# Releasing loads at two points of a step, one-hot rows queued by step, and narrower weight subtractions, in a fused attention and expert kernel

## The chip, the cores and the metric

The kernel runs on one core of a Trainium2 chip. The core has five engines with a queue each: PE (matrix multiplies and transposes, results in eight PSUM banks ps0 to ps7), DVE (vector work), ACT (activations and copies), POOL (the general engine, which also issues indirect DMAs) and SP (which here only issues DMAs). Every queue runs in its own order; an instruction that has to wait holds up all that stand behind it on the same engine. The metric is the device time of one execution in microseconds (us); lower is better.

## The reference

Eight batches, eight heads, 512 local and 32 global tokens, head size 64. Local tokens attend to a window of 32 to each side and to the global ones; global tokens attend to all. The result, 4352 tokens of width 512, goes into a mixture of eight experts with a "sticky" choice: a token takes its own best expert when its local gate is under 0.5, otherwise that of the token before.

```python
    s_g = scale * np.matmul(q_g, k_all.transpose(0, 1, 3, 2))
    out_g = np.matmul(sm(s_g), v_all)
    s_ll = scale * np.matmul(q_l, k_l.transpose(0, 1, 3, 2))
...
    mask = np.abs(pos[:, None] - pos[None, :]) <= window
    s_ll = np.where(mask, s_ll, -1000000000.0)
...
    s_l = np.concatenate([s_lg, s_ll], axis=-1)
    a_l = sm(s_l)
    out_l = np.matmul(a_l, np.concatenate([v_g, v_l], axis=2))
...
            fresh_e = int(np.argmax(logits[b, s]))
            if s == 0 or local_gate[b, s] < 0.5:
                e = fresh_e
            else:
                e = prev_e if prev_e >= 0 else fresh_e
...
            h = np.maximum(x[b, s] @ w1[e], 0.0)
            out[b, s] = p[e] * (h @ w2[e])
```

## The kernel before

**Attention.** `Attn.run` walks 48 units in 48 steps s = 0 to 47. A batch is six units: l0, l1, g0, l2, g1, l3, where an l unit is a pair of heads for the local tokens and a g unit is the global tokens of two pairs. A step starts unit s (scores, maximum, subtraction, exponential) and finishes unit s - 2 (transposes of the exponentials, product with v, division). In the order in which a step is written: the loads, `prep`, the transposes of unit s - 2 (`l_t` or `g_t`, L264 and L332), some pieces of the gate computation of earlier batches, the scores of unit s (`l_s`, L247, in two halves; or `g_s`, L300) with the maxima, and the product with v (`l_av`, `g_av`, L280 and L343). The order of the text is the order on each engine.

**Loads.** At the top of an l step, `load` (L178) fetches q and k of the pair two ahead into the ring `raw` of four buffers, and `loadv` (L188) fetches v of the next pair into the ring `v` of four. SP issues them in order; each waits only until its buffer is free, so SP can run ahead of the steps. `prep` makes the tiles `qbd` and `kx` of the next pair from `raw` with six instructions on POOL (L191). These tiles have two buffers, so `prep` of a pair waits for the scores of the pair two before it.

**Routing.** Small instructions of the routing come from generators that `drip` advances between the instructions of a step. `stage_a` handles the first five batches (CA = 21 columns of 128 tokens) while attention still runs: it ranks the tokens by expert, and builds in `low` one one-hot row block of 128x128 for each column in the tile `o1` (printed as o). POOL makes all 21 (L916), in the order in which `drip` comes to them. `pick` then multiplies the 21 blocks with a second one-hot table on PE (L1013), which gives the list idx of rows that the first expert blocks gather.

**Experts.** A weight is used as a sum of two parts: `split` makes the upper one by a cast on ACT (L1164, `hi`), `flush` the lower one by a subtraction (L1174, `lo`), 1024 columns wide. The first two weights of the first block are subtracted on POOL, in `pre` during the last steps of attention; all others on DVE. `mm1` multiplies hi with the upper part of x, lo with it, and hi with the lower part of x, 12 matmuls of 128x256 into one PSUM bank from the ring `ph`; `early` runs the first NX = 3 blocks, in the first of which the leftovers of attention (the generator `tail`: transposes L332, products L343, L280) are interleaved. The ring `ph` starts with ps2; ps0 to ps2 are also the banks of the attention scores, ps3 is the bank of the gate pieces. `ps_63` to `ps_70` in the listings below are ps0 to ps7. Behind that come eleven and more expert blocks of the same kind.

## Time and profile before

| | |
|---|---|
| median of 3 runs | 690.34 us (688.4 to 693.82) |
| the profiled execution | 690.5 us |
| its span, first to last instruction | 688.8 us |
| PE busy, share of the span | 659.1 us, 96% |
| DVE, ACT, POOL busy | 425.9, 343.0, 212.0 us |
| mean granted PE clock | 0.984 |
| attention ends, expert blocks begin | about 224 us |

The profile names engines, lines of the source and tiles. Columns of a timeline are start and length in us, engine, line, operation, out<-in, shapes and count; in brackets stands how long the engine was idle before and what ended that. Rows of time windows give busy us of PE, weight loads (PEld), DVE, ACT and POOL, then the granted PE clock, the busy share of the DMA engines and GB/s. A row of waits gives total us, times, and the longest.

### The profile page before, as it was taken

How to read it: one execution, taken by the hardware profiler on the slowest of the kernel's cores; microseconds unless marked ns; L12 is line 12 of the kernel's file. 1: busy time of each engine (PE TensorE's matmuls, PEld its weight loads, DVE VectorE, ACT ScalarE, POOL GpSimd, SP SyncE). 2: the span in 40 equal slices, each digit the busy share in tenths (PEclk: the TensorE clock that was granted, in tenths of full speed). 3: DMA queues.
4: the chain of work that ended last, by engine and by line, in shares of the span. 5: the costliest groups of instructions: out<-in, count | busy, mean ns of one | idle time of the engine just before them, and what ended most of it. 6: DMA issues, size and time to landing. Idle time of an engine off the chain costs nothing.

```text
span 688.8 us, 18451 instructions
## 1 busy us (share of the span) xinstructions
PE 659.1 (96%) x7253; PEld 566.6 (82%) x7253; DVE 425.9 (62%) x1050; ACT 343.0 (50%) x614; POOL 212.0 (31%) x342
## 2 busy tenths in 40 slices
PE   8999999999979799998998999999999999999995
PEld 7788788877767788887887988889898889888994
DVE  7878787777877777994517636325354516255573
ACT  4565565664646474653326635344444325255563
POOL 7734434343674211132022403040403020133023
PEclk9999999999999899999998999999999999999998
DMA  8957977979576486878319547347466417265673
GB/s 334 362 210 258 335 257 276 346 279 332 177 285 227 158 309 234 264 247 277 125 60 320 196 161 244 101 130 230 149 213 194 146 57 230 68 227 177 226 272 103
DMA packets 43012, 151.45 MB, mean 220 GB/s; under 512 B 7965, under 2 KB 9245, under 8 KB 38688
## 3 DMA queue, kind: packets, MB, share of 16 engines
q1 hardware_dynamic: 30928, 118.25, 49.4%
q0 software_dynamic: 6960, 21.90, 9.6%
q10 hardware_dynamic: 4896, 8.80, 3.5%
q8 instruction: 78, 1.28, 0.8%
q14 instruction: 150, 1.23, 0.6%
HBM read 130.55 MB, written 19.69 MB: 218 GB/s over the span
## 4 chain that ended last, share of the span: by engine, by line
PE 80%; DVE 10%; POOL 4%; issue 4%; ACT 1%; POOLq 0%; ACTq 0%; DVEq 0%
PE ps L1276 27%; PE ps L1265 25%; PE ps L247 7%; PE ps L264 4%; PE ps L280 3%; PE ps L1219 3%; PE ps L300 2%; POOL o L916 2%; PE ps L356 2%; PE ps L343 2%; DVE wp L1174 2%; PE ps L332 1%; DVE wq L1174 1%; PE ps L371 1%; PE ps L236 1%
## 5 line engine op out<-in xcount | busy, mean ns | idle before, releaser
L1282 POOL DMA_INDIRECT out_dram<-y,tk x39 | 42.9, 1100 | 315.1 <-ACT y L1281 232.7
L1276 PE MATMUL ps<-wp,wq 128*128 128x512 f32 x504 | 129.5, 404 | 1.0 <-ACT wq L1379 1.0
L1276 PEld LDWEIGHTS ps<-wp,wq 128*128 128x128 f32 x504 | 94.1, 192 | 21.3 <-ACT wq L1379 1.3
L1265 PE MATMUL ps<-wp,wp 128*128 128x256 f32 (+5 forms) x672 | 109.3, 322 | 0.3 <-issue 0.3
L1265 PEld LDWEIGHTS ps<-wp,wp 128*128 128x128 f32 x672 | 103.6, 188 | 5.3 <-issue 0.4
L1268 DVE SCALAR_TENSOR_TENSOR wq<-ps,wq 128x256 fp32r<-128x256 f32 (+5 forms) x80 | 41.7, 525 | 73.8 <-ACT wq L1267 66.4
L1267 ACT ACTIVATE wq<-ps 128x256 fp32r<-128x256 f32 (+5 forms) x80 | 37.3, 469 | 79.1 <-PE ps L1265 69.4
L1222 DVE TENSOR_TENSOR wp<-ps,wp 128x512 fp32r<-128x512 f32 x40 | 27.6, 691 | 78.3 <-ACT wp L1221 78.2
L191 POOL TENSOR_SCALAR_AFFINE_SELECT qbd<-raw 64x512 f32<-64x512 f32 x62 | 44.4, 715 | 89.1 <-PE ps L247 69.7
L247 PE MATMUL ps<-kx,qbd 128*64 128x128 f32 x1024 | 65.9, 280 | 3.9 <-POOL kx L191 3.5
L247 PEld LDWEIGHTS ps<-kx,qbd 128*64 128x64 f32 x1024 | 56.6, 139 | 11.8 <-POOL kx L191 6.7
L1281 ACT ACTIVATE y<-ps,pp 128x512 f32<-128x512 f32 x39 | 26.9, 689 | 77.7 <-PE ps L1276 70.7
L252 DVE TENSOR_REDUCE mx<-ps 128x4 f32<-128x512 f32 x64 | 43.8, 685 | 32.0 <-PE ps L247 32.0
L258 ACT ACTIVATE pe<-pe 128x512 f32<-128x512 f32 x64 | 40.8, 638 | 43.3 <-DVE pe L254 43.3
L1174 DVE TENSOR_TENSOR wp<-raw,wp 128x1024 fp32r<-128x1024 f32 x47 | 56.9, 1217 | 2.9 <-ACT wp L1164 2.8
L1205 POOL DMA_INDIRECT xa<-xs,idx x42 | 52.3, 1245 | 16.3 <-issue 10.0
L1164 ACT CAST wp<-raw 128x1024 fp32r<-128x1024 f32 x49 | 50.9, 1047 | 2.7 <-DVE f L930 1.5
L1221 ACT CAST wp<-ps 128x512 fp32r<-128x512 f32 x40 | 23.4, 588 | 53.2 <-PE ps L1219 53.2
L254 DVE TENSOR_TENSOR pe<-ps,mx 128x512 f32<-128x512 f32 x64 | 43.9, 686 | 1.0
L191 POOL TENSOR_SCALAR_AFFINE_SELECT kx<-raw 128x384 f32<-128x384 f32 (+3 forms) x127 | 43.2, 373 | 2.9 <-DMA raw<-in_qk_dram 0.8
L266 ACT COPY pt<-ps 128x512 f32<-128x512 f32 x64 | 34.7, 600 | 9.8 <-PE ps L264 9.1
L280 PEld LDWEIGHTS ps<-v,pt 128*32 128x32 f32 x2048 | 32.0, 110 | 9.2 <-issue 6.5
(280 smaller groups left out, 1182.5 us busy)
## 6 DMA issues: line engine op xcount, KB each, us to landing
raw<-in_w_dram SPq DMA_DIRECT2D x78, 512.0 KB, 4.3
v<-in_vw_dram SPq DMA_DIRECT2D x32, 1040.0 KB, 7.9
raw<-in_qk_dram SPq DMA_DIRECT2D x32, 528.0 KB, 7.5
xa<-in_w_dram SPq DMA_DIRECT2D x26, 512.0 KB, 4.7
xT<-in_w_dram SPq DMA_DIRECT2D x20, 512.0 KB, 5.3
xs<-xa ACTq DMA_DIRECT2D x8, 1056.0 KB, 8.6
qgb<-in_qg_dram SPq DMA_DIRECT2D x8, 128.0 KB, 5.0
xa<-xs,idx POOLq DMA_INDIRECT x42, 4.9
```

The lines of the kernel that those rows point to most:

```text
L191: self.nc.gpsimd.affine_select(out=out, in_=in_, pattern=pat, compare_op=ALU.is_ge, fill=0.0, base=0, channel_multiplier=0)
L247: nc.tensor.matmul(sp[64 * t2:64 * t2 + 64, t], qbd[:, w], kf[:, f:f + P], start=False, stop=True, skip_group_check=True)
L252: nc.vector.tensor_reduce(out=mx, in_=st["sps"][hb], axis=AX.X, op=ALU.max)
L254: nc.vector.tensor_tensor(out=st["pe"][:, 4 * hb:4 * hb + 4], in0=st["sps"][hb], in1=mx.broadcast_to([P, 4, P]), op=ALU.subtract)
L280: nc.tensor.matmul(o[32 * w4:32 * w4 + 32, g, h], pt[:, 2 * g + w4 // 2, w4 % 2, h, :], v[:, w, h * (D + 1):(h + 1) * (D + 1)], start=True ...
L1164: nc.scalar.copy(out=hi, in_=raw)
L1174: (nc.gpsimd if pool else nc.vector).tensor_tensor(out=lo, in0=raw, in1=hi.bitcast(F32), op=ALU.subtract)
L1205: self.nc.gpsimd.indirect_dma_start(out=self.xr[j] if k == "early" else self.xr4[:, j], out_offset=None, in_=src, in_offset=bass.IndirectO ...
L1265: nc.tensor.matmul(ph, a[:, dc, fs], b_[:, dc, n0:n1], start=(n == 0), stop=(n == 11))
L1268: nc.vector.scalar_tensor_tensor(out=hl[:, fc, n0:n1], in0=ph, scalar=0.0, in1=hh[:, fc, n0:n1].bitcast(F32), op0=ALU.max, op1=ALU.subtract)
L1276: nc.tensor.matmul(py, a[:, fc, js], b_[:, fs], start=(fc == 0 and k == 0), stop=(fc == 7 and k == 2))
L1282: sc = nc.gpsimd.indirect_dma_start(out=self.out, out_offset=bass.IndirectOffsetOnAxis(ap=self.g[1][:, j:j + 1], axis=0), in_=y, in_offset ...
```

## The change

Five edits are in it.

1. `get` issues the loads of q, k and of v and, where `gate` is set, makes them wait for one PE instruction. The load of q and k of the pair two ahead now stands behind the transposes of the step and waits for the last of them; that of v of the next pair stands behind the first half of the scores and waits for its last matmul. SP's order of instructions stays as it was; each such row has one more wait, for PE.
2. Of the 21 one-hot blocks, the first CD = 6 are made on DVE, three in one instruction; the other 15 go in five entries of three into a list `pq`. A step takes one entry from it (a g step two) and puts it on POOL behind `prep`. `pick` does not go on to its matmuls until the list is empty.
3. The two subtractions on POOL are cut into four of 256 columns each.
4. The ring `ph` starts with ps3 in place of ps2.
5. `rt.pq` and `at.pq` are the same list.

```diff
 NX = 3
+CD = 6
 LISTS = "lists"
...
         self.cur = {}
+        self.gate = self.last = None
+        self.pq = []
         self.gens = []
...
     def load(self, b, pr):
-        nc = self.nc
         if pr == 0:
             self.cur[b] = {"v": []}
         c = self.cur[b]
         t = c[("qk", pr)] = self.ld()
-        nc.sync.dma_start(t, self.qk[b, pr])
+        self.get(t, self.qk[b, pr])
 
     def load_g(self, b):
         g = self.cur[b]["qg"] = self.qgb()
         self.nc.sync.dma_start(g, self.qg[b])
 
     def loadv(self, b, pr):
-        nc = self.nc
         v = self.v()
         self.cur[b]["v"].append(v)
-        nc.sync.dma_start(v.rearrange("p w c -> p (w c)"), self.vw[b, pr])
+        self.get(v.rearrange("p w c -> p (w c)"), self.vw[b, pr])
+
+    def get(self, out, in_):
+        d = self.nc.sync.dma_start(out, in_)
+        if self.gate is not None:
+            self.tc.add_manual_dep(d.ins, self.gate.ins.name, mybir.DependencyInfo(mybir.DependencyClass.Sync, mybir.DependencyReason.DATA), reason="pace")
 
...
                 f = 32 * (3 * (w // 2) + w % 2)
-                nc.tensor.matmul(sp[64 * t2:64 * t2 + 64, t], qbd[:, w], kf[:, f:f + P], start=False, stop=True, skip_group_check=True)
+                self.last = nc.tensor.matmul(sp[64 * t2:64 * t2 + 64, t], qbd[:, w], kf[:, f:f + P], start=False, stop=True, skip_group_check=True)
 
...
         for i in range(4):
-            nc.tensor.transpose(tp[:, i], st["pe"][:, 4 * hb + i], self.cst.idf)
+            self.last = nc.tensor.transpose(tp[:, i], st["pe"][:, 4 * hb + i], self.cst.idf)
         pt = self.pt()
...
             for i in range(3):
-                nc.tensor.transpose(tp[:, i], st["pg"][:, c0 + i], self.cst.idf)
+                self.last = nc.tensor.transpose(tp[:, i], st["pg"][:, c0 + i], self.cst.idf)
             nc.scalar.copy(out=pt[:, c0:c0 + 3], in_=tp[:, 0:3])
...
             sg = st is not None and not sl
+            ahead = pairs[npr + 1:npr + 3] if nl else []
             if nl:
-                if npr + 2 < len(pairs):
-                    b, i = pairs[npr + 2]["u"]
-                    self.load(b, i)
-                    if i == 0:
-                        self.load_g(b)
-                if npr + 1 < len(pairs):
-                    self.loadv(*pairs[npr + 1]["u"])
                 npr += 1
                 if npr < len(pairs):
                     self.prep(pairs[npr])
+            for _ in range(2 - nl):
+                if self.pq:
+                    self.pq.pop(0)()
             if sl:
                 self.l_t(st, 0)
                 self.l_t(st, 1)
             if sg:
                 self.g_t(st)
+            self.gate = self.last
+            if len(ahead) > 1:
+                b, i = ahead[1]["u"]
+                self.load(b, i)
+                if i == 0:
+                    self.load_g(b)
             if nl:
...
                 self.l_s(nx, 0)
+                self.gate = self.last if s > 0 else None
+                if ahead:
+                    self.loadv(*ahead[0]["u"])
                 self.l_max(nx, 0)
...
         yield from self.rank2(0, CA)
-        for c0 in range(0, CA, 3):
-            yield from self.low(c0, min(c0 + 3, CA), True)
+        for c0 in range(0, CD, 3):
+            yield from self.low(c0, c0 + 3, False)
+        for c0 in range(CD, CA, 3):
+            self.pq.append(lambda c0=c0: all_(self.low(c0, min(c0 + 3, CA), True)))
         yield PSUM
...
         yield from lag(wait)
+        while self.pq:
+            yield
         yield PSUM
...
         self.add([buf.tile([P, 2048], F32R, name=f"wp{k}") for k in range(2)])
-        self.ph, self.py, self.xtp = Ring(ps[2:4]), Ring(ps[0:2]), Ring(ps[4:6])
+        self.ph, self.py, self.xtp = Ring([ps[3], ps[2]]), Ring(ps[0:2]), Ring(ps[4:6])
         self.xt0 = None
...
             pool, raw, hi, lo = self.pend.pop(0)
-            (nc.gpsimd if pool else nc.vector).tensor_tensor(out=lo, in0=raw, in1=hi.bitcast(F32), op=ALU.subtract)
+            m = 4 if pool else 1
+            for k in range(m):
+                f = slice(1024 // m * k, 1024 // m * (k + 1))
+                (nc.gpsimd if pool else nc.vector).tensor_tensor(out=lo[:, f], in0=raw[:, f], in1=hi[:, f].bitcast(F32), op=ALU.subtract)
             if not any(raw is x for x in self.gone):
...
     at.at1, at.at2 = s1, s2
+    rt.pq = at.pq
     at.run(rt, moe)
```

Line numbers of the changed file are 6 to 19 higher in the places below. On POOL, around the seventh batch (raw_80 holds its fourth pair, raw_77 the first of the eighth batch), the order before is:

```order
L191 AFFINE_SELECT kx_146<-raw_79 128x7x32
L916 TENSOR_SCALAR o_290<-io_261,plo 128x128 [waits DVE_49]
L916 TENSOR_SCALAR o_290<-io_261,plo 128x128 x11
L191 AFFINE_SELECT qbd_145<-raw_80 64x16x32 [waits DMAHW5_49,PE_49]
L191 AFFINE_SELECT qbd_145<-raw_80 64x16x32 [waits Pool_49]
L191 AFFINE_SELECT kx_147<-raw_80 128x128 [waits Pool_49]
L191 AFFINE_SELECT kx_147<-raw_80 128x6x64
L191 AFFINE_SELECT kx_147<-raw_80 128x32
L191 AFFINE_SELECT kx_147<-raw_80 128x7x32
L916 TENSOR_SCALAR o_290<-io_261,plo 128x128 x9
L191 AFFINE_SELECT qbd_144<-raw_77 64x16x32 [waits DMAHW7_49,PE_49]
```

And now:

```order
L197 AFFINE_SELECT kx_147<-raw_80 128x7x32
L930 TENSOR_SCALAR o_290<-io_261,plo 128x128 [waits DVE_49]
L930 TENSOR_SCALAR o_290<-io_261,plo 128x128 x5
L197 AFFINE_SELECT qbd_144<-raw_77 64x16x32 [waits DMAHW7_49,PE_49]
L197 AFFINE_SELECT qbd_144<-raw_77 64x16x32 [waits Pool_49]
L197 AFFINE_SELECT kx_146<-raw_77 128x128 [waits Pool_49]
L197 AFFINE_SELECT kx_146<-raw_77 128x6x64
L197 AFFINE_SELECT kx_146<-raw_77 128x32
L197 AFFINE_SELECT kx_146<-raw_77 128x7x32
L930 TENSOR_SCALAR o_290<-io_261,plo 128x128 x3
L197 AFFINE_SELECT qbd_145<-raw_78 64x16x32 [waits DMAHW2_49,PE_49]
```

The groups of 12 and 9 have become 6, 3, 3 and 3, the first behind the `prep` of raw_80, the last behind that of raw_79 of the eighth batch (its pair l2).

On PE, the index matmuls of `pick` stood behind the scores of the global unit g0 of the eighth batch (raw_77 and raw_78 with qgb):

```order
L363 MATMUL ps_66<-idf,xg_111 128x128
L300 MATMUL ps_64<-raw_77,qgb_153 64x256 [waits DMAHW7_49,DMAHW0_49]
L300 MATMUL ps_64<-raw_78,qgb_153 64x256 [waits DMAHW2_49]
L300 MATMUL ps_65<-raw_77,qgb_153 64x288 [waits DVE_49]
L300 MATMUL ps_65<-raw_78,qgb_153 64x288
L1013 LDWEIGHTS o_290
L1013 MATMUL ps_70<-oe,o_290 128x12 [waits DVE_49]
```

Now they stand between the two halves of the scores of the pair before it, l1 (kx_147 made from raw_78), and the last six of their weight loads wait for POOL; the last of these and what follows:

```order
L1029 LDWEIGHTS o_290 [waits Pool_49]
L1029 MATMUL ps_70<-oe,o_290 128x12
L253 MATMUL ps_63<-kx_147,qbd_145 64x128 x8
L286 MATMUL ps_69<-v_136,pt_142 32x65 [waits DVE_49,Activation_49]
L286 MATMUL ps_69<-v_136,pt_142 32x65 x15
```

They moved ahead by most of a step, past the product with v and the transposes of the next step.

Also on PE, the first matmuls of the first expert block (wp_100 is the first split weight, xh and xl the parts of x) before:

```order
L280 MATMUL ps_69<-v_135,pt_141 32x65 x15
L1265 MATMUL ps_65<-xh,wp_100 128x256 [waits DVE_49]
L1265 MATMUL ps_65<-xh,wp_100 128x256 x3
L1265 MATMUL ps_65<-xh,wp_100 128x256 [waits Pool_49]
L1265 MATMUL ps_65<-xh,wp_100 128x256 x3
L1265 MATMUL ps_65<-xl,wp_100 128x256 x4
L332 MATMUL ps_68<-idf,pg_149 128x128 x3
```

And now:

```order
L286 MATMUL ps_69<-v_135,pt_141 32x65 x15
L1284 MATMUL ps_66<-xh,wp_100 128x256 [waits Activation_49]
L1284 MATMUL ps_66<-xh,wp_100 128x256 x3
L1284 MATMUL ps_66<-xh,wp_100 128x256 [waits Pool_49] x4
L1284 MATMUL ps_66<-xl,wp_100 128x256 [waits DVE_49]
L1284 MATMUL ps_66<-xl,wp_100 128x256 x3
L338 MATMUL ps_68<-idf,pg_149 128x128 x3
```

The first matmul waits for ACT where it waited for DVE, and each of the four with lo waits for its own quarter of the subtraction.

## The prediction

> **What bounds the kernel now.** I read the page's first part and chain, then windows of 20 us for stretches in which PE is not full.
>
> ```profile
> PE 659.1 (96%) x7253; PEld 566.6 (82%) x7253; DVE 425.9 (62%) x1050; ACT 343.0 (50%) x614; POOL 212.0 (31%) x342
> PE 80%; DVE 10%; POOL 4%; issue 4%; ACT 1%; POOLq 0%; ACTq 0%; DVEq 0%
> 160.00:180.00 20.00, 18.89 (x419) 15.71 (x419) 16.92 (x63) 10.53 (x24) 7.45 (x16) 1.00 0.77 277
> 180.00:200.00 20.00, 16.46 (x348) 13.22 (x348) 15.82 (x55) 8.37 (x20) 19.09 (x37) 0.91 0.75 276
> 220.00:240.00 20.00, 16.06 (x249) 15.01 (x248) 14.56 (x37) 10.87 (x21) 5.67 (x3) 0.83 0.52 181
> ```
>
> PE sets the time; only its idle time, and time at a reduced clock, can be won. Most of attention looks like the first window (1.1 us idle in 20). Two windows, 180:200 and 220:240, have 3.5 and 3.9 us idle and also a clock below 1.00. POOL is busy for 19.1 of 20 us in the first of them. The timeline there:
>
> ```profile
> 178.11 7.00 POOL L916 TENSOR_SCALAR o<-io,plo 128x128 bf16<-128x128 bf16 x12 [8.87 <-DVE plo L899]
> ...
> 178.84 1.97 PE L247 MATMUL ps<-kx,qbd 128*64 128x128 f32 x32
> ...
> 187.62 2.17 PE L247 MATMUL ps<-kx,qbd 128*64 128x128 f32 x32
> ...
> 187.97 5.24 POOL L916 TENSOR_SCALAR o<-io,plo 128x128 bf16<-128x128 bf16 x9
> ...
> 191.70 0.60 PE L356 MATMUL ps<-idf,xa 128*128 128x128 f32 x4
> ...
> 193.16 1.49 POOL L191 TENSOR_SCALAR_AFFINE_SELECT qbd<-raw 64x512 f32<-64x512 f32 x2
> ...
> 194.73 1.50 POOL L191 TENSOR_SCALAR_AFFINE_SELECT kx<-raw 128x128 f32<-128x128 f32 x4
> ...
> 195.24 0.44 PE L247 MATMUL ps<-kx,qbd 128*64 128x128 f32 x4 [2.94 <-POOL kx L191]
> ...
> 196.28 3.25 PE L247 MATMUL ps<-kx,qbd 128*64 128x128 f32 x28 [0.60 <-POOL kx L191]
> ...
> 196.00:198.00 2.00, 1.72 (x16) 1.72 (x18) 0.13 (x1) 0.00 (x0) 1.87 (x5) 0.52 1.01 396
> ```
>
> Stall A: the scores of the eighth batch's l0 are next from 192.3 (end of L356), and wait 2.94 us for a `prep` queued on POOL behind nine one-hot blocks. The 32 score matmuls, 1.97 us elsewhere, then run from 195.24 to 199.53, 4.29 us, the clock being 0.52. Lost: 2.94 + (4.29 - 1.97) = 5.3 us.
>
> Stall B is at the change to the expert blocks:
>
> ```profile
> 222.53 3.03 DVE L741 TENSOR_TENSOR leq<-leq,ro 128x40 f32<-128x40 f32 x1
> 222.68 1.12 PE L280 MATMUL ps<-v,pt 128*32 128x65 f32 x64
> 223.14 2.36 POOL L1174 TENSOR_TENSOR wp<-raw,wp 128x1024 fp32r<-128x1024 f32 x1
> ...
> 226.79 0.69 DVE L254 TENSOR_TENSOR pe<-ps,mx 128x512 f32<-128x512 f32 x1
> ...
> 227.54 2.07 PE L1265 MATMUL ps<-xh,wp 128*128 128x256 f32 x8 [3.74 <-DVE pe L254]
> ...
> 235.12 1.21 PE L1265 MATMUL ps<-xh,wp 128*128 128x256 f32 x8
> 236.17 0.64 PE L1265 MATMUL ps<-xl,wp 128*128 128x256 f32 x4
> ...
> L741 DVE TENSOR_TENSOR leq<-leq,ro x8: 190/195/3028, 51.6 to 256.4; 128x40 f32<-128x40 f32 x8
> ...
> 228.00:230.00 2.00, 2.00 (x11) 2.00 (x11) 1.68 (x8) 1.22 (x3) 0.84 (x1) 0.50 0.14 53
> ```
>
> A DVE instruction of 0.195 us lasted 3.03 us and ended with the 1024-wide subtraction on POOL. The scores' subtraction behind it (L254) ended at 227.48, and only then was ps2 free for the first expert matmul. From the end of the product with v, 223.80, to the third group of twelve matmuls at 235.12, PE did two such groups, six transposes and 48 small products in 11.3 us, much of it at clock 0.50. At full clock these are 2 x 1.7 (235.12 to 236.81), 0.9 for the transposes (the row of L332 below) and 48/64 of 1.12 for the products: 5.1 us. Lost: 6.2 us.
>
> **The change part by part.** Prices come from this execution (690.5 us, 0.16 above the median of 690.34).
>
> *One-hot blocks.*
>
> ```profile
> L916 POOL TENSOR_SCALAR o<-io,plo x21: 592/595/622, 178.1 to 192.6; 128x128 bf16<-128x128 bf16 x21
> ...
> L919 DVE TENSOR_TENSOR o<-io,plo x3: 554/818/819, 288.1 to 289.5; 128x640 bf16<-128x640 bf16 x2, 128x384 bf16<-128x384 bf16 x1
> ```
>
> POOL loses 6 x 0.6 = 3.6 us; DVE gains two instructions of 0.55 us (the 128x384 form), 1.1 us, hidden behind the two steps that a subtraction has until its transposes. Behind each `prep` now stand at most 1.8 us of one-hots, and `prep` of the eighth batch's l0 follows six of them instead of twelve, a `prep` and nine: 178.1 + 3.6 = 181.7, so its tiles are there by 184.7, and the scores want them at 192.3. Stall A goes.
>
> What is late next is the index product. It now stands between the halves of the scores of l1 and needs the last three blocks, which stand behind `prep` of l2, which needs the load of l2, which now waits for the transposes of step l0:
>
> ```profile
> 190.77 0.87 PE L332 MATMUL ps<-idf,pg 128*128 128x128 f32 x6
> ...
> raw<-in_w_dram SPq DMA_DIRECT2D x78, 512.0 KB, 4.3
> v<-in_vw_dram SPq DMA_DIRECT2D x32, 1040.0 KB, 7.9
> raw<-in_qk_dram SPq DMA_DIRECT2D x32, 528.0 KB, 7.5
> ```
>
> On the time axis of before: the transposes end at 191.6, the load is issued at 191.8 and lands 4.3 (a weight of nearly this size) to 7.5 us later (the median of these loads), 196.1 to 199.3. `prep` takes 2.9 us (193.16 to 196.1 for its six rows), three blocks 1.8: ready at 200.8 to 204.0. PE, freed of stall A, comes to the last three blocks at 198.2 (scores from 192.3; 4.4 us to the next pair's, half of the 8.78 us between the two L247 rows of 178.84 and 187.62, which lie two steps apart; 1.0 for a half; an estimated 0.5 for the first 18 blocks). New wait: 2.6 to 5.8 us. I take 2.6, since the bursts that make 7.5 are gone by then; a v of twice the size just ahead of it speaks for more. A: 5.3 - 2.6 = 2.7 us won, bounds -2.2 (5.8, and 4.29 - 1.97 - 0.60 = 1.7 for a cold clock) to 5.3.
>
> By the Trainium skill, TensorE: Matmul & The Clock Gate, the section on HAM oscillation, the clock suffers from PE gaps of more than about 3.4 us, so a wait of 2.6 would cost no clock. The row has 2.94 us of idle, a little work and 0.60 more, with 0.52 behind it; that neither contradicts the page nor makes 2.6 safe.
>
> *Narrower subtractions and the first bank.* A quarter takes at least 2.36/4 = 0.59 us; the fixed part is unknown, and I take 0.7, a bit above the 0.6 of a 128-wide one-hot. Starting at 223.14, quarters end at 223.8 to 225.9. DVE can wait for one quarter, not for 2.36 us, so L254 ends near 225.7. PE starts on ps3 at 223.80, if ACT's copy out of it is done, meets the last quarter at 225.9, and ends the first group about 1.0 later than it could. The second group finds ps2 free; the products behind it wait for ACT, which casts the second weight first: about 1.0 more. Left of 6.2 are 2.0: B wins 4.2 us, bounds 2 (a late weight, below) to 6.2.
>
> *The loads.* The waits are on SP, and what stands behind them there are the next loads and the stores of xg. Are the loads still early enough?
>
> ```profile
> 102.03 1.09 PE L264 MATMUL ps<-idf,pe 128*128 128x128 f32 x8
> ...
> 113.51 1.97 PE L247 MATMUL ps<-kx,qbd 128*64 128x128 f32 x32
> ...
> 129.24 0.38 SPq L178 DMA_DIRECT2D raw<-in_qk_dram  x1
> ...
> 138.86 1.50 POOL L191 TENSOR_SCALAR_AFFINE_SELECT qbd<-raw 64x512 f32<-64x512 f32 x2 [3.44 <-DMA raw<-in_qk_dram]
> ```
>
> The tightest is l1 of each batch: issued behind the transposes of l3 (103.1), wanted at 113.5 less 2.9 for `prep`, 7.4 us later. At 4.3 us there is room of 3.1; at 7.5 none; at the 9.6 of the last two rows, behind a burst, 2.2 is lost each batch. When it is issued now, the previous loads are 7 us old, so I take 5 and no loss. The v loads have three steps. What can be won are PE's waits that nothing in the profile explains:
>
> ```profile
> PE ps L343 <- issue: 2.8, 3, 1.2
> PE ps L264 <- issue: 1.3, 2, 0.8
> PE ps L356 <- issue: 0.7, 1, 0.7
> 74.00:75.00 1.00, 0.75 (x36) 0.54 (x35) 0.90 (x4) 0.04 (x1) 0.00 (x0) 1.00 0.99 382
> ```
>
> They are 4.8 us in attention and fall where the DMA engines are full, as in the last row, which suggests instructions fetched late. Evenly spread loads carry as many bytes, so some full stretches stay; between 0 and 4.8 I take 1.0.
>
> The Trainium skill, DMA: Bandwidth & Descriptors, Queues, rings and completion order, speaks against this gain: a DMA engine serves its queue rows in turn, packet by packet, so a fetch would not wait behind the depth of SP's row. By that the term is 0 and the sum 683.6; no row here shows the turns.
>
> The last loads also move the weights: the last v of all now waits for scores that lie about 8 us (two steps less half the scores) ahead of the step in which ACT casts the first weight, and that weight stands behind it on SP.
>
> ```profile
> 207.30 24.58 SPq L1154 DMA_DIRECT2D raw<-in_w_dram  x6
> ...
> 220.40 1.09 ACT L1164 CAST wp<-raw 128x1024 fp32r<-128x1024 f32 x1
> ```
>
> So its issue goes from 207.3 to about 213.3 (212.4 and 1 for the instructions between), and it lands 4.3 to 7.9 later (the second if v's landing counts for it), 217.6 to 221.2, for a cast at 220.4: 0 to 0.8 us, and I take 0.
>
> Sum: 2.7 + 4.2 + 1.0 = 7.9 us off 690.5, 682.6; the later blocks are PE-bound and pass it on.
>
> **The rivals.**
> - *Issue waits gone*: all 4.8 us. 690.5 - 2.7 - 4.2 - 4.8 = 678.8. For it: their place at full DMA; against: the bytes are the same. Chance 0.13.
> - *No gain from pacing*: the core moves as many bytes in as many full stretches, and the issue waits stay. 690.5 - 6.9 = 683.6. Chance 0.15. The Trainium skill's rule above comes to the same.
> - *The index product takes back stall A*: load at 7.5 us, wait 5.8, perhaps cold: A gives -0.5, cold -2.2. With the rest 690.5 + 0.5 - 4.2 - 1.0 = 685.8, cold 687.5. For it: DMA share of 1.01 at 196:198. Chance 0.18.
> - *The first weight or its bank is late*, B gives 2: 690.5 - 2.7 - 2 - 1.0 = 684.8. Chance 0.08.
> - *Slower: the load of l1 late in every batch.* Seven batches at (landing - 7.4) us. It breaks even at 7.9/7 + 7.4 = 8.5 us and is 1% slower from 9.5. At 10.5 us it costs 21.7: 704. For it: the row of 9.6; against: that load stood in a burst, which the change breaks up. Chance 0.11.
> - That a gate does nothing is excluded for nearly all loads: their rows on SP have a new wait for PE.
>
> **How the numbers follow.** Forecast 682.6, chance 0.35. About 1%, 6.9 us, is what a measurement can tell from no change: 683.4 and 697.2 are the bounds. Faster: 0.25 of the forecast's, 0.13, 0.07 of the case without a gain from pacing, 0.03 of the rest: 0.48. Slower: 0.10. Same: 0.42. The range runs from 677 (issue waits gone) to 690 (index product and weight late together), leaving out the slow rival and little else.
>
> **What would show it.** POOL's one-hots in groups of 6, 3, 3, 3 and no PE wait for kx near 192; a PE wait for o at the index product of about 2.6 us (the term that I trust least); L741 and L769 under 1 us; the first expert matmul within 0.5 us of the last product with v, clock 1.00 behind it; landings of qk near 5 us and no PE wait for kx at l1. The prediction is wrong if PE waits for kx once a batch, or if the clock falls at the index product.

## The result, and the profile after

The kernel before took 690.88 us (median; 687.88 to 694.98), the changed kernel 696.44 us (692.87 to 702.59): 1.008 of it, 95% interval 1.0058 to 1.0102. The change makes the kernel about 5.6 us slower, where the prediction had it 7.9 us faster. The profiled execution of the changed kernel is the slowest of its twenty, 702.59 us (span 700.9), so its sums are too large by some 6 us; a second profile, nearer to the median, comes with the experiments. One execution each of the two kernels with copies below (700.7 and 701.27 us) is more than 1.5% above the fastest of its kernel, and the ratios leave it out.

The busy times and, in the same columns as in the prediction, five windows of 20 us of the changed kernel:

```profile
PE 663.3 (95%) x7253; PEld 569.5 (81%) x7253; DVE 425.7 (61%) x1052; ACT 344.1 (49%) x614; POOL 208.0 (30%) x342
...
40.00:60.00 20.00, 17.42 (x340) 14.47 (x330) 10.58 (x36) 8.99 (x22) 5.76 (x13) 0.83 0.46 148
160.00:180.00 20.00, 15.11 (x308) 11.91 (x304) 12.23 (x48) 8.20 (x19) 5.71 (x13) 0.89 0.80 288
180.00:200.00 20.00, 19.46 (x400) 15.74 (x392) 16.35 (x56) 10.58 (x23) 12.06 (x25) 0.94 0.52 182
...
220.00:240.00 20.00, 19.34 (x413) 15.26 (x404) 15.91 (x55) 13.10 (x31) 7.21 (x12) 1.00 0.66 234
240.00:260.00 20.00, 17.30 (x223) 16.54 (x224) 13.04 (x34) 11.23 (x20) 2.81 (x4) 0.91 0.60 191
```

The two weak windows of before (180:200 and 220:240) have filled up. In their place stand others with idle time and a clock below 1.00: 40:60, 160:180 (4.9 us idle) and 240:260. PE's waits up to the expert blocks, longest sums first:

```profile
PE ps L836 <- ACT ptg L339: 3.8, 1, 3.8
PE ps L349 <- ACT ptg L339: 3.2, 2, 2.7
PE ps L286 <- issue: 3.0, 2, 2.6
PE ps L377 <- ACT xT L363: 2.7, 4, 1.1
PE ps L270 <- issue: 2.1, 2, 1.1
PE ps L349 <- issue: 1.9, 2, 1.4
PE ps L362 <- issue: 1.5, 1, 1.5
...
PE ps L1029 <- POOL o L930: 0.8, 2, 0.4
PE ps L1284 <- POOL wp L1193: 0.6, 2, 0.3
```

No wait for kx is left, and the two waits that the prediction feared, for the one-hot rows (L1029, 0.8 us) and for the first weight (L1284, 0.6 us), are small. What has grown is PE's wait for ACT, 9.7 us in the three rows with L339 and L363, where before had 1.3; and the issue waits (idle time of PE for which the profile shows no cause), 8.5 us in four rows, which the pacing was to shorten from 5.1 (the prediction's 4.8 and a row of 0.3).

The first and the last group of the one-hots on POOL, the last product with v and the first expert matmul, and the landings of q, k and of v:

```profile
193.23 3.63 POOL L930 TENSOR_SCALAR o<-io,plo 128x128 bf16<-128x128 bf16 x6 [3.45 <-DVE plo L913]
...
214.56 1.76 POOL L930 TENSOR_SCALAR o<-io,plo 128x128 bf16<-128x128 bf16 x3
...
236.67 1.12 PE L286 MATMUL ps<-v,pt 128*32 128x65 f32 x64
237.72 1.31 PE L1284 MATMUL ps<-xh,wp 128*128 128x256 f32 x6
...
v<-in_vw_dram SPq DMA_DIRECT2D x32, 1040.0 KB, 7.3
raw<-in_qk_dram SPq DMA_DIRECT2D x32, 528.0 KB, 5.3
```

So the change does what it says: groups of six and three, expert matmuls right behind the last product, landings of 5.3 us where 7.5 stood. DVE's instruction of 3.03 us before (L741, now L753) takes at most 0.78 us.

### The profile page after: what moved, and what is told of

Its sections match the earlier page's. It is cut to its first block, busy times and chain, and to the rows that moved or that the text cites. A ratio compares the mean times of both kernels' runs of the same rounds, so it can differ in the third digit from the quotient of the medians.

```text
span 700.9 us, 18467 instructions
## 1 busy us (share of the span) xinstructions
PE 663.3 (95%) x7253; PEld 569.5 (81%) x7253; DVE 425.7 (61%) x1052; ACT 344.1 (49%) x614; POOL 208.0 (30%) x342
## 4 chain that ended last, share of the span: by engine, by line
PE 56%; DVE 6%; issue 1%; ACT 1%; POOL 0%; POOLq 0%; DVEq 0%; ACTq 0%
PE ps L1295 27%; PE ps L1284 25%; PE ps L1238 2%; DVE wp L1193 1%; DVE wq L1193 1%; PE ps L1407 1%; DVE hl L1287 1%; DVE xT L1019 0%; DVE xT L1017 0%; DVE o L933 0%; POOL xa L1224 0%; DVE xl L1241 0%; PE ps L270 0%; PE ps L1029 0%; PE ps L362 0%
## 5 line engine op out<-in xcount | busy, mean ns | idle before, releaser
L1284 PE MATMUL ps<-wp,wp 128*128 128x256 f32 (+5 forms) x672 | 109.3, 322 | 0.3 <-issue 0.3
L1284 PEld LDWEIGHTS ps<-wp,wp 128*128 128x128 f32 x672 | 103.6, 188 | 5.4 <-issue 0.5
L1286 ACT ACTIVATE wq<-ps 128x256 fp32r<-128x256 f32 (+5 forms) x80 | 37.3, 469 | 77.4 <-PE ps L1284 73.4
L260 DVE TENSOR_TENSOR pe<-ps,mx 128x512 f32<-128x512 f32 x64 | 43.9, 686 | 1.0
```

The lines of the kernel that those rows point to most:

```text
L260: nc.vector.tensor_tensor(out=st["pe"][:, 4 * hb:4 * hb + 4], in0=st["sps"][hb], in1=mx.broadcast_to([P, 4, P]), op=ALU.subtract)
L1284: nc.tensor.matmul(ph, a[:, dc, fs], b_[:, dc, n0:n1], start=(n == 0), stop=(n == 11))
```

## The experiments

All ratios are to the kernel before, run beside them on the same chip (its median there 692.3 to 692.6 us).

Theory P at the start: the waits of the loads cost more than 10 us, the other parts win what was predicted. Theory R: the other parts win nothing.

**The changed kernel again.**

> The changed kernel once more, beside the three below, and for a profile nearer to its median than the first one (702.59 us against 696.44). Every theory expects 695 to 698 us. If the added time is a matter of waits that come by chance (PE's issue waits), their places and sizes differ from the first profile (2.6 us at 40 us, 3.8 us for ACT at 173 us); if it is a matter of the order of the program, the second issue of a store on ACT (gx, line 431) comes again 0.5 to 3.2 us behind the first (xa, line 426), where it came 0.4 to 0.5 us behind it in the kernel before.

Measured: 698.81 us (696.48 to 702.31), ratio 1.0100 (1.0065 to 1.0135). The profiled execution has a span of 695.4 us. The issue wait near 40 us is there again (2.06 us), and so is the long wait for ACT near 170 us (2.91 us), the store of gx 0.5 to 2.6 us behind that of xa. The loss has fixed places.

**Without the waits of the loads.**

```
             if sg:
                 self.g_t(st)
-            self.gate = self.last
+            self.gate = None
...
                 self.l_s(nx, 0)
-                self.gate = self.last if s > 0 else None
+                self.gate = None
```

> The changed kernel with the loads where they now stand in the program, but without the wait of a load for the transposes or scores. Theory P (the pacing costs the time, the other parts win what the prediction said, 6.9 us): 683 to 686 us, issue of gx 0.5 us behind xa again, PE's waits for ACT's copies (line 339, 363) under 2 us from 9.7. Theory R (one-hots by step and narrow subtractions win nothing and cost): 695 to 698 us, as the changed kernel. Both in part: 688 to 692 us.

Measured: 688.67 us (684.96 to 692.01), ratio 0.995 (0.9926 to 0.9975). The waits of the loads cost 1.0100 - 0.995 = 1.5%, 10.4 us; by the two intervals that is sure to some 3 us either way. The other parts win 3.5 us, half of the 6.9 predicted: theory P in the main, with smaller gains.

**The waits of the loads alone.** The kernel before with loads moved and made to wait, one-hots, subtractions and bank as before. Of the change these edits stay (with `get` and the places that set `last`):

```
+            self.gate = self.last
+            if len(ahead) > 1:
+                b, i = ahead[1]["u"]
+                self.load(b, i)
...
+                self.gate = self.last if s > 0 else None
+                if ahead:
+                    self.loadv(*ahead[0]["u"])
```

> The kernel before with the loads moved and made to wait as in the changed kernel; one-hots, subtractions and the first bank as before. Theory P: the wait costs 10 us or more, 700 to 704 us. Theory R: 689 to 692 us. Both in part: 694 to 698 us.

Measured: 701.02 us (698.4 to 702.7), ratio 1.0115 (1.0088 to 1.0143): theory P's number.

Where the time goes shows when one instruction is followed through the profiles. Each attention step has two subtractions of the maximum on DVE (L254 before, L260 after), 64 in all. The table has the start of some of them in before, and how much later (us) they start in four other kernels. Its last line is the fifth activation of the expert blocks on ACT (L1267 before, L1286 in the changed kernel), behind which the difference changes little (spans: 688.8 before; 6.6, 5.6 and 12.1 more, and 2.8 less).

```
                    before    changed,   gx first   waits of     changed, no
                    starts    again      (below)    loads alone  waits of loads
subtraction 11       35.07     +0.3       +0.9       -0.3         +1.4
subtraction 13       43.01     +2.7       +5.1       +3.7         +1.4
subtraction 47      160.06     +4.2       +5.7       +3.8         -0.1
subtraction 51      171.54     +7.7       +6.1       +8.1         -0.1
subtraction 55      189.75     +9.0       +7.0       +8.1         +1.2
subtraction 59      203.87     +6.2       +4.1       +9.1         -3.0
subtraction 63      225.48     +5.6       +3.5      +12.6         -3.7
expert activation   241.36     +6.6       +4.6      +12.5         -2.7
```

Each column is one profile. Wherever loads wait, 2.4 to 4.2 us are lost between 35 and 43 us, and (but for the kernel with gx first) another 3.6 to 4.3 between 160 and 172 us. Stall A is won between 190 and 204 us by all with the new one-hots; the kernel with waits alone keeps both old stalls. The 1.4 us that the kernel without waits of loads has lost by 35 us are an issue wait of 1.36 us at 31.26 us.

**The second place: ACT, and the transfer eight back.** SP's loads, ACT's queue and PE in the changed kernel (the second profile), near 165 us:

```profile
163.42 0.33 SPq L192 DMA_DIRECT2D v<-in_vw_dram  x1
...
167.56 0.37 ACTq L426 DMA_DIRECT2D xs<-xa  x1
...
169.81 0.32 ACTq L431 DMA_DIRECT2D xs<-gx  x1
170.17 0.86 ACT L339 COPY ptg<-ps 128x384 f32<-128x384 f32 x2 [4.61 <-DMA v<-in_vw_dram]
...
170.71 0.49 PE L836 MATMUL ps<-idf,key 128*5 128x128 f32 x3 [2.91 <-ACT ptg L339]
```

And the same place in the kernel without the waits of loads:

```profile
155.55 0.33 SPq L192 DMA_DIRECT2D v<-in_vw_dram  x1
...
162.92 0.37 ACTq L426 DMA_DIRECT2D xs<-xa  x1
163.38 0.46 ACTq L431 DMA_DIRECT2D xs<-gx  x1
...
164.42 0.60 PE L836 MATMUL ps<-idf,key 128*5 128x128 f32 x4 [0.83 <-ACT ptg L339]
```

ACT issues the store of gx right behind that of xa in the second, 2.25 us later in the first, and the copy of ptg, for which PE waits, stands behind it. The name in the bracket says for what: a load of v. The two have no data in common. The transfers of SP and ACT share eight semaphores in turn, and each issue waits for the transfer that had its semaphore before, the eighth one back. In the built program of the changed kernel, the two rows on ACT with the semaphores that they wait for:

```
L426 DMA xs<-xa_109 128x4x528 [waits DMAHW7_49,DVE_49]
L431 DMA xs<-gx 32x16 [waits DMAHW4_49,DVE_49]
```

The transfer that had DMAHW4 last is the load of v issued at 163.42: between them come two of xg's stores, xa, two more of xg, a load of q and k, and one of v. In the kernel before and in the one without waits, the eighth one back is that v as well, but there it is issued as early as SP finds room: without waits at 155.55 us, 7.8 ahead of gx, and its last landing is at 160.46, 2.9 ahead of gx. Made to wait for scores, it starts only 4.1 us ahead of xa's issue (163.42 to 167.56), and its last landing is at 169.74; gx is issued at 169.81. In the first four batches the eighth one back is a store of xg, which SP issues behind loads that wait. The landings in the trace bear the rule out: in the second profile each of the first six stores of gx is issued 0.02 to 0.08 us after the last landing on its semaphore, in the kernel without waits of loads 1.7 to 3.6 us after it.

By the Trainium skill, DMA: Bandwidth & Descriptors, Anatomy of one DMA, a DMA engine doesn't wait on semaphores; the issuing sequencer does, ahead of dispatch. The trace agrees: it is ACT that stands, for 2.25 us, with a ready copy behind it.

Two kernels take this wait away. One moves that store to SP's queue:

```
-        nc.scalar.dma_start(xsg[:, DM:ROW], rt.gx[rq])
+        nc.sync.dma_start(xsg[:, DM:ROW], rt.gx[rq])
```

> The changed kernel with the small store of gx issued on SP's queue, not on ACT's. What it tells apart is where the pacing costs, if it does. Theory P1 (ACT stands at that issue until an earlier load has landed, and PE waits for the copy behind it): 690 to 693 us, PE's waits for ACT's copies under 2 us. Theory P2 (PE's issue waits and the clock behind them, wherever the DMA engines are full): 695 to 698 us, PE's waits for ACT gone all the same.

Measured: 694.08 us (690.79 to 697.9), ratio 1.0016 (0.9992 to 1.0041), although it has a new and larger wait of its own. PE's longest one in it, and the load on which that hangs:

```profile
PE ps L1029 <- POOL o L930: 6.2, 3, 5.4
...
196.39 0.31 SPq L431 DMA_DIRECT2D xs<-gx  x1
196.81 1.96 SPq L192 DMA_DIRECT2D raw<-in_qk_dram  x1
...
203.56 1.49 POOL L197 TENSOR_SCALAR_AFFINE_SELECT qbd<-raw 64x512 f32<-64x512 f32 x2 [5.76 <-DMA raw<-in_qk_dram]
```

On SP the store waits in front of a load of q and k, which lands 6.8 us after 196.81; `prep` and the last three one-hots follow, and the index product waits 5.4 us. That is the prediction's rival for stall A, close to the 5.8 us that it put on the wait; it comes about where SP is held up once more, and not in the changed kernel.

The other issues gx ahead of the five stores of its batch, so that the eighth one back is older (here a load of q and k that landed at 156.19 us, 13 us ahead of gx):

```
         r0 = P * (1 + gcol(hf)) + 32 * b4
         xsg = self.xs[r0:r0 + 32]
+        nc.scalar.dma_start(xsg[:, DM:ROW], rt.gx[rq])
         r0 = P * (1 + col(b))
...
-        nc.scalar.dma_start(xsg[:, DM:ROW], rt.gx[rq])
```

> The changed kernel with the store of gx issued ahead of those of xa and xg, still on ACT. Theory P1 (ACT stands at that issue until one of the last loads has landed): ahead of the five other stores it comes after loads that landed long ago, so ACT doesn't stand; 4 to 6 us less than the changed kernel (1.006 of it is the 694.08 us of the run before with gx on SP, which paid a wait of 5.4 us at the index product instead), ratio to before 1.001 to 1.004. Theory P2 (PE's issue waits alone): no gain, ratio 1.008 to 1.01. Both theories: the issue wait of about 2 us near 41 us stays.

Measured: 692.79 us (689.18 to 697.98), ratio 1.0007 (0.998 to 1.0035). PE's wait for the copy ahead of L836 falls from 2.9 to 0.8 us, and 0.93%, 6.4 us, come back, most of the pacing's 10.4: theory P1. By the intervals this 6.4 is sure to some 3 us.

A wait of loads is not the only thing that makes ACT stand there. The one-hots alone (below), in whose kernel no load waits, have the same wait of PE in their profile, which is of the slowest of their twelve executions:

```profile
166.78 2.19 ACTq L431 DMA_DIRECT2D xs<-gx  x1
...
169.54 0.60 PE L836 MATMUL ps<-idf,key 128*5 128x128 f32 x4 [2.57 <-ACT ptg L339]
```

There gx is issued right behind xa, but the issue itself takes 2.19 us, where it takes 0.46 in the kernel without waits of loads. Why is open.

**Only q and k wait.** The wait for the scores is left out, that for the transposes stays.

```
-                self.gate = self.last if s > 0 else None
+                self.gate = None
```

> The changed kernel with the loads of v not waiting for the scores; those of q and k still wait for the transposes. If ACT's stand at gx is for a load of v that waits, it goes, and so does half of the pacing: ratio 1.000 to 1.003. If it is for a load of q and k, or if the pacing costs by both alike, ratio 1.006 to 1.01. Without any wait of a load the ratio was 0.995, with both 1.010.

Measured: 698.21 us (695.24 to 701.91), ratio 1.0086 (1.0055 to 1.0118). Within the intervals one wait is as bad as two: the load of v stands on SP behind a load of q and k that waits. In the profile v is issued at 164.90 us, right behind q and k (164.53), and gx at 172.33, 2.1 us behind xa; PE waits 2.7 us for the copy.

**The first place: instructions that come late.** The changed kernel (second profile) from 38 to 40 us, and then the kernel without waits of loads. The last three columns are the clock, the DMA share and GB/s (a DMA packet counts in the window in which it starts, so a share can pass 1):

```profile
38.00:39.00 1.00, 1.00 (x32) 0.49 (x32) 0.94 (x6) 1.00 (x3) 0.00 (x0) 1.00 0.99 417
39.00:40.00 1.00, 0.85 (x57) 0.70 (x47) 0.96 (x5) 0.07 (x2) 0.79 (x2) 1.00 1.02 424
...
41.91 0.31 PE L286 MATMUL ps<-v,pt 128*32 128x65 f32 x5 [2.06 <-issue]
```

```profile
38.00:39.00 1.00, 1.00 (x11) 0.76 (x11) 1.00 (x6) 0.74 (x2) 0.93 (x4) 1.00 0.00 0
39.00:40.00 1.00, 1.00 (x32) 0.49 (x32) 0.94 (x6) 1.00 (x3) 0.58 (x3) 1.00 0.00 0
```

Loads that may start at once come in bursts and leave the DMA engines idle behind them, here from 38 to 40 us. Loads that wait fill this hole. Six profiles of kernels whose loads wait all have an issue wait of 1.8 to 2.6 us at this product with v; those of the kernel before and of the kernel without waits have none. Theory F takes this for a late fetch of PE's instructions. To see whether full DMA engines are enough, the hole was filled in the kernel without waits, by copying the seventh load of v once, or twice, more to memory that nothing reads:

```
         self.get(v.rearrange("p w c -> p (w c)"), self.vw[b, pr])
+        if (b, pr) == (1, 2):
+            for k in range(1):
+                self.nc.sync.dma_start(self.dm[k], self.vw[b, pr])
```

> The changed kernel without any wait of a load, and one transfer more: behind the seventh load of v (issued at 33.0 us) its 1040 KB are copied once more, to memory that nothing reads. In the profile of that kernel the DMA engines stand idle from 37 to 41 us, and PE has no issue wait there; in six profiles of kernels whose loads wait they are full until 39 to 40 us, and PE has an issue wait of about 2 us at the product with v near 40 us. Theory F (PE's next instructions are fetched in that stretch and come late behind full DMA engines): with the copy the engines are full until about 40 us or later, and the issue wait of 1.8 to 2.6 us is there at 39 to 42 us, though no load waits; ratio 0.997 to 1.002. Theory G (the issue wait comes of the order or the waits of the loads as such): no issue wait there, ratio 0.994 to 0.997.

> The same with two such copies. Theory F: the full stretch ends some 2.6 us (or more) later, and the issue wait grows by as much, to 4 to 6 us, with a lower clock behind it; ratio 1.000 to 1.006. If the fetch is only slowed by other transfers, not kept until they end, it stays near 2 us. Theory G: none, ratio 0.994 to 0.997.

Measured with one copy: 691.68 us (687.14 to 700.7), ratio 0.9971 (0.994 to 1.0001); with two: 693.92 us (690.26 to 701.27), ratio 1.0023 (0.9989 to 1.0057). PE at that product (its line is three further down here), with one and with two:

```profile
41.31 0.31 PE L289 MATMUL ps<-v,pt 128*32 128x65 f32 x5 [1.51 <-issue]
```

```profile
42.26 0.31 PE L289 MATMUL ps<-v,pt 128*32 128x65 f32 x5 [1.91 <-issue]
```

The issue wait appears at the same instruction though no load waits. With two copies the time is 5.0 us longer than without (ratio 1.0023 to 0.995), with one 1.5 us, which lies within the intervals; where the 5 us are lost stays open, since the profile, of an execution near the lowest time, has little more than this one wait.

That it is a fetch shows in the trace's single DMA packets. The profile counts a queue of the kind "instruction" with packets of 16 KB; its row in the second profile:

```profile
q8 instruction: 78, 1.28, 0.7%
```

One such packet ends 1.2 to 1.5 us before PE goes on, in all nine profiles that have the wait at this product (in the second profile it runs from 39.49 to 40.46 us, PE goes on at 41.91; with one copy from 38.92 to 39.88, PE at 41.31). Without waits of loads it starts at 37.66 us, right after the loads' packets have ended, and PE doesn't wait. With two copies it runs from 39.96 to 41.06 us between packets of the copies on its DMA engine, with two of them still behind it, so it isn't always kept until the queue is empty.

"Full DMA engines" says too much, though. The ninth profile is that of the fastest kernel (the last of this section), in which no load waits and nothing is copied:

```profile
38.00:39.00 1.00, 1.00 (x10) 0.48 (x8) 0.94 (x8) 1.00 (x4) 1.00 (x3) 1.00 0.06 25
39.00:40.00 1.00, 1.00 (x64) 0.80 (x64) 1.00 (x3) 0.52 (x1) 0.07 (x1) 1.00 0.10 33
...
42.15 0.31 PE L286 MATMUL ps<-v,pt 128*32 128x65 f32 x5 [1.78 <-issue]
```

A share of 0.06 is one engine of sixteen. In the packets one engine still works off load packets, one after the other, until 39.84 us, and at that moment the fetch starts; PE passed at 37.16 the matmul at which the fetch starts in the kernel without waits. So one engine that is behind is enough, if the fetch is on it. And up to this point the fastest kernel has the same program as the kernel without waits of loads, so the wait can come or not in one program: of the six profiles in which up to here no load waits and nothing is copied (before, without waits of loads, and four that follow) one has it; of the six with waits, all.

**Waits of loads from the fourteenth step on, gx first.** The same edit as with gx first, and in both places that set the gate:

```
-            self.gate = self.last
+            self.gate = self.last if s > 12 else None
```

> The changed kernel with the store of gx first, and with loads that wait only from the fourteenth step on (about 57 us), so not in the stretch ahead of the issue wait near 40 us. If ACT's stand at gx and that one issue wait are what the pacing costs, this comes out as the kernel without waits of loads: ratio 0.994 to 0.998. If issue waits come up everywhere that loads wait, it stays near the run with gx first: 0.999 to 1.002.

Measured: 690.66 us (687.39 to 693.95), ratio 0.9978 (0.9952 to 1.0004). Its profile has no issue wait near 40 us, but one of 2.45 us at 31.65, where no load waits yet. Another 0.29%, 2.0 us, are back, but the intervals of this kernel and of the one with gx first overlap. Of the pacing's 10.4 us, ACT's wait is 6.4; how the other 4.0 split between the fetch near 40 us and other places is not shown.

**The one-hots alone, the subtractions and the bank alone.** Each with the loads where they were. Of the change the first has

```
-        for c0 in range(0, CA, 3):
-            yield from self.low(c0, min(c0 + 3, CA), True)
+        for c0 in range(0, CD, 3):
+            yield from self.low(c0, c0 + 3, False)
+        for c0 in range(CD, CA, 3):
+            self.pq.append(lambda c0=c0: all_(self.low(c0, min(c0 + 3, CA), True)))
```

(and what takes the blocks from the queue in each step), the second

```
-        self.ph, self.py, self.xtp = Ring(ps[2:4]), Ring(ps[0:2]), Ring(ps[4:6])
+        self.ph, self.py, self.xtp = Ring([ps[3], ps[2]]), Ring(ps[0:2]), Ring(ps[4:6])
...
+            m = 4 if pool else 1
+            for k in range(m):
```

> The kernel before with the one-hot rows queued by step, and nothing else. By the prediction stall A (5.3 us) goes and an index wait of up to 2.6 comes: 2.7 to 5.3 us less than before, ratio 0.992 to 0.996. Theory R (the stall is replaced by another at once): ratio 0.998 to 1.002.

> The kernel before with the subtractions on POOL 256 columns wide and the other first bank, and nothing else. By the prediction stall B loses 4.2 of its 6.2 us: ratio 0.992 to 0.995. Rival: four quarters hold up DVE's next instructions one by one, ACT's issue of xa waits for them and PE for the copy behind it (2.7 us in the profile of the kernel whose loads don't wait): 1 to 2 us won, ratio 0.997 to 0.999.

Measured: one-hots 689.85 us (686.55 to 694.92), ratio 0.9961 (0.9943 to 0.9979), 2.7 us won. Subtractions and bank 690.31 us (687.96 to 691.87), ratio 0.9957 (0.994 to 0.9974), 3.0 us won, less than the 4.2 predicted; beside the one-hots they add only 0.11% (0.9961 to 0.995). That the two together win 3.5 us and not 5.7 lies about within the intervals. What the subtractions lose stands some 4 us behind stall B's place, in their own profile as in this one of the kernel without waits of loads (PE's wait is 2.66 us in both):

```profile
225.51 2.80 POOL L1193 TENSOR_TENSOR wp<-raw,wp 128x256 fp32r<-128x256 f32 x4 [0.96 <-ACT wp L1180]
...
227.00 0.65 DVE L787 TENSOR_TENSOR gx<-lpr,lsu 32x8 f32<-32x8 f32 x1
227.66 0.67 DVE L790 COPY xa<-tok 128x4 int32<-128x4 int32 x1
...
228.39 0.40 ACTq L426 DMA_DIRECT2D xs<-xa  x1
228.89 0.46 ACTq L431 DMA_DIRECT2D xs<-gx  x1
...
230.20 1.53 PE L349 MATMUL ps<-v,ptg 128*32 128x65 f32 x48 [2.66 <-ACT ptg L339]
```

Four quarters of 0.70 us follow each other on POOL, and of DVE's small steps beside them four are stretched: L781, L785, L787 and L790 take 0.43, 0.46, 0.65 and 0.67 us and end at 226.26, 226.99, 227.65 and 228.33, each within 0.1 us of the end of a quarter (226.21, 226.91, 227.61 and 228.31 if all are equally long). In an earlier batch, where POOL runs no subtraction, L787 and L790 take 0.17 and 0.15. ACT stands at the stores of xa and gx for those steps, and PE waits 2.66 us for the copy behind them. If that is so, it helps to issue the stores of this one batch on SP, which has nothing urgent there:

```
+        q = nc.sync if b == 6 else nc.scalar
-        nc.scalar.dma_start(self.xs[r0:r0 + 4 * P] ...
+        q.dma_start(self.xs[r0:r0 + 4 * P] ...
...
-        nc.scalar.dma_start(xsg[:, DM:ROW], rt.gx[rq])
+        q.dma_start(xsg[:, DM:ROW], rt.gx[rq])
```

> The changed kernel without any wait of a load, and with the stores of the seventh batch's xa and gx issued on SP's queue instead of ACT's. In the profile without waits of loads ACT stands there until 228.5 us for DVE, whose small steps each wait for a quarter of POOL's subtraction, and PE waits 2.66 us for the copy behind it. By that reading the wait goes, and with it 2.7 us and a colder clock behind: 2.5 to 4 us off, ratio 0.989 to 0.992. If the wait only moves to DVE's or POOL's next work: 0.994 to 0.996.

Measured: 684.54 us (683.69 to 685.69), ratio 0.9878 (0.9842 to 0.9913), the fastest kernel of all: 8.4 us under before, and 5.0 under the kernel without this edit, more than the 2.5 to 4 that were expected. The same place in it, and its window of 20 us, which had 16.96 us of PE at 0.91 without the edit:

```profile
228.19 0.86 ACT L339 COPY ptg<-ps 128x384 f32<-128x384 f32 x2
...
229.36 0.65 DVE L788 TENSOR_TENSOR gx<-lpr,lsu 32x8 f32<-32x8 f32 x1
...
229.83 0.89 PE L349 MATMUL ps<-v,ptg 128*32 128x65 f32 x48
...
220.00:240.00 20.00, 19.62 (x327) 17.99 (x327) 16.59 (x52) 14.51 (x28) 6.63 (x9) 1.00 0.64 218
```

DVE is as slow as before, but nothing that PE needs stands behind it any more, and the clock stays at 1.00.

## Why the prediction was wrong

**The loads: this step failed.** It took 1.0 us of gain and no loss; measured are 10.4 us of loss.
- It asked how late a load may land by one reader alone, `prep` (7.4 us of room) and the product with v (three steps). That was right: q and k land in 5.3 us, "near 5", and PE never waits for kx. The slower rival rested on this reader too, and its mechanism didn't come about; only its sign did.
- Of what stands behind the waits it named SP's next loads and the stores of xg, and stopped at SP. The landing of a load also releases a semaphore, for which the transfer eight later waits on whatever queue it is issued; that one is on ACT, in front of a copy that PE needs. 6.4 us.
- It read that the issue waits fall where the DMA engines are full, and drew from it that even loads shorten them; in the first profile they grew from 5.1 to 8.5 us. The bursts left holes, and in one of them lay a fetch that made no wait. With loads that wait it comes behind load packets and costs PE 1.8 to 2.6 us in all six profiles. The rule of turns that the prediction set against a gain is seen once, with two copies; in the fastest kernel the fetch comes behind seven load packets of its engine, counted from 37.16 us, and when it was asked for is not recorded. The bounds "between 0 and 4.8" shut out a loss without a reason, and that made the whole range too low: it ended at 690.

**Stall A: the mechanism right, the sum by luck.** The groups and the missing wait for kx are as predicted, and so is the gain (2.7 us, measured 2.7 alone, interval 1.5 to 3.9). But the term that it trusted least, the index product's wait of 2.6 us, is 0.8 us, so 4.5 should have been won. Between 189.75 and 203.87 us the kernel without waits of loads does win 4.2 (the table); it loses 1.4 ahead of 35 us in the issue wait at 31.26, which the prediction has no term for. Whether that is what made the one-hots alone win less is not shown.

**Stall B: the place right, the size not.** The first expert matmul starts with the end of the last product, in full clock, as predicted. The step "DVE can wait for one quarter" failed: it can wait for one again at the next instruction, and beside the next weight's four quarters in a row four instructions do so. So the wait for DVE came back 4 us later, through ACT's queue: 3.0 us won alone instead of 4.2 (which is the end of the interval, 1.8 to 4.2), and 5.0 more when the stores leave that queue.

## What to carry to other kernels

Before a transfer is held back, list everything that its landing releases: the readers of its data, and the later transfers that take turns with it on semaphores, on every queue that issues them; a compute engine that issues such a transfer stands still with all that is queued behind it. A hole in the DMA share is not waste as such: spreading loads evenly can push instruction fetches out of it, so look at which fetches make no wait now, and look at single DMA engines, since a mean share of 0.06 can hide the one that matters. And cutting a blocking instruction in four helps little where the other engine runs many small instructions beside it; what pays is to take the dependent issue out of the queue that the bound engine waits for.

## What the runs showed of the hardware that was not expected

A wait of about 2 us at the same instruction leaves the clock at 1.00 in one execution and halves it in another. In the changed kernel (second profile; 2.06 us of wait) and in the kernel with waits of loads alone (2.15 us), two windows just behind it:

```profile
43.00:44.00 1.00, 1.00 (x13) 0.81 (x13) 0.10 (x1) 0.82 (x2) 0.00 (x0) 1.00 0.06 16
```

```profile
43.00:44.00 1.00, 1.00 (x7) 0.67 (x5) 0.00 (x0) 0.59 (x1) 0.00 (x0) 0.50 0.54 50
```

At this instruction the clock stays at 1.00 behind waits of 1.51 to 2.06 us (five profiles) and halves behind those of 2.15 to 2.62 (four). That is no limit for other places: in the kernel whose loads wait from the fourteenth step on, 2.45 us at 31.65 leave it at 1.00. This may be a part of why executions of kernels with more such waits spread more (688 to 695 us before, 693 to 703 changed, 684 to 686 in six executions of the fastest kernel); it was not tested.

By the Trainium skill, Runtime: NRT & Kernel Launch, Instruction fetch mechanics, each sequencer refills its instructions by a DMA queue of its own, at a cost that is mostly hidden. The trace agrees on the queue (q8, in packets of 16 KB). In these runs the one near 40 us costs PE 1.5 to 2.6 us in the nine profiles in which its packet starts late, and nothing in the kernel without waits of loads, where it starts at 37.66 us.
